# Three column tiles for two products, first keys in two transfers and output weights in ten, in a decoding step with a sliding window

## The chip, the cores and the metric

The kernel runs on one core of a Trainium2 chip. Times are microseconds (us) of the device for one execution. The question is one of some tenths of a microsecond in 191, so a few terms are read from single records of the trace: when an instruction began, when a transfer's packet ran on a DMA engine, when a transfer's completion raised its semaphore. No view of the profile prints these; they were read from the packed traces. Profiled spans are shorter than the timed execution.

## The reference, cut to what matters

```python
def _A_ref(x, k_cache, v_cache, wq, wo):        # x (8, 1, 448), caches (8, 8, 4096, 256)
    W = 1024                                    # window
    q = (x @ wq) ...                            # 16 heads of 256
    k, v = the last W rows of the caches, each of 8 heads used twice
    p = softmax(q k^T / 16);  o = p v
    return o.reshape(8, 1, 4096) @ wo           # wo (4096, 448)
def _B_ref(x, w1, b1, w2, b2):
    return gelu(layernorm(x) @ w1 + b1) @ w2 + b2
g = sigmoid((x * gate_w).sum(-1))
out = g * _A_ref(...) + (1 - g) * _B_ref(...)   # (8, 1, 448), bf16
```

The step reads 77.7 MB and writes 7 KB.

## The kernel before

All large loads go through one ring of nine slots of 2 MB and are issued by SP in one order: query weights, first keys, MLP weights, then keys and values by turns, and the output weights last. The output weights are four quarters, two to a slot. The first three quarters are one transfer each; the last is cut 4+2+2 (of eight row blocks) so that the projection can begin on its first half.

```python
    OT = 4
    DO = D // OT                                              # 112 columns
    WO_PARTS = [[(0, NJ8)]] * (NHQ - 1) + [[(0, 4), (4, 6), (6, 8)]]
    ...
    add_kv("k", A_k_cache, 0)                                 # one transfer of 2 MB
    ...
    for q in range(0, NHQ, 2):
        add(("wo", q), rows_loader(
            [wo_v[:, q + i, j0 * D : j1 * D] for i in range(2) for j0, j1 in WO_PARTS[q + i]]))
    ...
    def tiles(ps):                                            # four column tiles, at partitions 0, 32, 64, 96
        return [(ps[32 * i : 32 * i + NB, :], slice(i * DO, (i + 1) * DO)) for i in range(OT)]
    ...
    def project(q):
        for j in range(NJ8):
            for dst, cols in tiles(A_ps):
                nc.tensor.matmul(dst, lhsT=oP[:, j, q, :], rhs=w[:, o + cols.start : o + cols.stop], ...)
    ...                                                       # spread, values, projection of the quarters
    nc.vector.scalar_tensor_tensor(res[:], in0=A_ps[:], scalar=gg_s[:, 0:1], in1=mixb[:], ...)
    for i, (src, cols) in enumerate(tiles(res)):              # four stores, two by SP and two by ACT
        eng = nc.sync if i % 2 == 0 else nc.scalar
        eng.dma_start(out_f[:, cols], src)
```

Each transfer raises a semaphore when it has landed, and the compiled program hands eight such semaphores to the transfers in turn. And after the last store, the compiled program makes SP wait, one after the other, for all of them, in a fixed order.

Of the kernel before, what the change touches and what calls it, by code (L numbers as in the profile page):

```python
# [11 lines left out]
BF16 = mybir.dt.bfloat16  # L12
# [6 lines left out]
def kernel(  # L19
# [16 lines left out]
    P = nc.NUM_PARTITIONS  # L36

    NB, Sq, D = A_x.shape
# [15 lines left out]
    HH = HD // 2  # L54
    PAIR = 2
    OT = 4
    DO = D // OT
    QN = 512
    QUAD = 4
    RQ = QUAD * rep  # L60
# [7 lines left out]
    HPQ = 4  # L68
    NHQ = Hq // HPQ
    NJ8 = HPQ * NJ  # L70
    WO_PARTS = [[(0, NJ8)]] * (NHQ - 1) + [[(0, 4), (4, 6), (6, 8)]]
    RING = 9
    LAG = 2
    NK = 4
# [10 lines left out]
    consts = ctx.enter_context(tc.tile_pool(name="consts", bufs=1))  # L85
# [23 lines left out]
    def kv_loader(src, u, parts):  # L109
        b, half = divmod(u, Hkv // QUAD)  # L110
        v = src[b, half * QUAD : (half + 1) * QUAD, kv_base:Sk, :].rearrange(
            "a (s c) d -> s a (c d)", c=NCK
        )

        def load(t):
            n = NCK * Dh // parts
            for i in range(parts):
                nc.sync.dma_start(
                    t[:, i * n : (i + 1) * n], v[:, :, i * n : (i + 1) * n]
                )  # L120

        return load

    def rows_loader(pieces):
        def load(t):
            o = 0
            for ap in pieces:
                n = 1
                for s in ap.shape[1:]:
                    n *= s  # L130
                dst = t[:, o : o + n]
                if len(ap.shape) == 3:
                    dst = dst.rearrange("p (a n) -> p a n", a=ap.shape[1])
                nc.sync.dma_start(dst, ap)
                o += n

        return load
# [3 lines left out]
    def add(key, loader):  # L141
        index[key] = len(plan)
        plan.append(loader)

    def add_kv(name, src, u, parts=1):
        add((name, u), kv_loader(src, u, parts))
# [7 lines left out]

    add(("wq", 0), rows_loader([wq_m[:, 0 : 2 * HD]]))
    add(("wq", 1), rows_loader([wq_m[:, 2 * HD : 3 * HD], wq_t]))
    add_kv("k", A_k_cache, 0)
    add(("w1",), rows_loader([w1_m, w1_t]))
    add(("w2",), rows_loader([w2_v]))
    for u in range(1, NQ):  # L160
# [5 lines left out]
    for q in range(0, NHQ, 2):  # L166
# [5 lines left out]
                    for i in range(2)  # L172
                    for j0, j1 in WO_PARTS[q + i]
                ]
# [3 lines left out]
    def slot(*key):  # L178
        return slots[index[key]]

    consts.tile([P, 448], BF16, name="pad")
    x_sb = consts.tile([NB, D], BF16)
    pump()
    nc.scalar.dma_start(x_sb[:], xf)
# [18 lines left out]

    def tiles(ps):
        return [
            (ps[32 * i : 32 * i + NB, :], slice(i * DO, (i + 1) * DO))
            for i in range(OT)
        ]

    xz = consts.tile([NB, 2, P], BF16)  # L210
# [19 lines left out]
    ones_r = consts.tile([1, NB], BF16)  # L230
    mixb = consts.tile([P, DO], F32)
    res = consts.tile([P, DO], BF16)
    nc.vector.memset(spread[:], 0.0)
# [279 lines left out]
    def gather(u):  # L513
        first = soft.pop(u)
        os_ = epool.tile([P, Dh], F32, tag="os", name="os_")
        nc.vector.scalar_tensor_tensor(
            os_[:],
            in0=PO[:, 1, :],
            scalar=own[:, 1:2],
            in1=first[:],  # L520
            op0=ALU.mult,
            op1=ALU.add,
        )
        soft[u] = os_
# [61 lines left out]
    def mlp_out(hs):  # L586
        bb = ps_misc.tile([P, DO], F32, tag="misc", name="bb")
        nc.vector.memset(bb[:], 0.0)
        for c in range(NF):
            w = slot("w2")  # L590
            for dst, cols in tiles(bb):
                nc.tensor.matmul(
                    dst,
                    lhsT=hs[:, c, :],
                    rhs=w[:, c * D + cols.start : c * D + cols.stop],
                    start=(c == 0),
                    stop=False,
                )
        for dst, cols in tiles(bb):
            nc.tensor.matmul(  # L600
                dst, lhsT=ones_r[:], rhs=b2_r[:, cols], start=False, stop=True
            )
        done()
        nc.scalar.activation(mixb[:], bb[:], ACT.Copy, scale=gg_s[:, 1:2])
# [27 lines left out]
    u = NQ - 1  # L632
    A_ps = ps_misc.tile([P, DO], F32, tag="misc", name="A_ps")
    gather(u - 2)
# [32 lines left out]
    def project(q):  # L667
        w = slot("wo", q - q % 2)
        for j in range(NJ8):
            o = ((q % 2) * NJ8 + j) * D  # L670
            for dst, cols in tiles(A_ps):
                nc.tensor.matmul(  # L672
                    dst,
                    lhsT=oP[:, j, q, :],
                    rhs=w[:, o + cols.start : o + cols.stop],
                    start=(q == 0 and j == 0),
                    stop=(q == NHQ - 1 and j == NJ8 - 1),
                )
# [52 lines left out]
```

## Time and profile before

| | before |
|---|---|
| time, median of 3 (later groups: 191.03, 191.20, 191.22, 191.16) | 190.97 us |
| profiled span | 189.4 us |
| DMA queues, mean share of the 16 engines | 97% |
| last piece of output weights lands | 185.18 us |
| result is ready, stores are issued | 186.0 us |

From the page of the kernel before: engines (busy us, share, instructions) and the DMA queues with their packets, MB and share of the 16 engines.

```profile
PE 130.9 (69%) x1022; PEld 66.9 (35%) x1022; DVE 128.0 (68%) x186; ACT 43.2 (23%) x91; POOL 5.0 (3%) x7
...
DMA  6999999999999999999999999999999999999980
...
DMA packets 6590, 77.85 MB, mean 411 GB/s; under 512 B 929, under 2 KB 1330, under 8 KB 1970
...
q1 hardware_dynamic: 6368, 77.67, 96.6%
q8 instruction: 8, 0.13, 0.2%
q10 hardware_dynamic: 210, 0.02, 0.1%
q14 instruction: 4, 0.03, 0.0%
```

The row of digits is the DMA engines' busy share in 40 slices: they are busy throughout, and no other engine is. (PE is TensorE, which does the matmuls, PEld its weight loads, DVE VectorE, ACT ScalarE and POOL GpSimd. SP is SyncE, which in this kernel only issues transfers and waits.) The two "instruction" queues carry the engines' own programs.

From the chain of waits of the kernel before, in order of time (start, duration, what):

```profile
129.78 37.00 DMA slot<-in_A_v_cache_dram
...
166.79 18.39 DMA slot<-in_A_wo_dram
185.18 0.04 issue
185.22 0.39 PE A_ps L672 x6
185.61 0.03 issue
185.63 0.33 DVE res L690
```

The chain stops at 185.96 us, at the last computing instruction. The span ends at 189.4. From the timeline of the kernel before, the stores; and from the list of waits of SP from 185.9 us on (waiter, released by: us in total, times, longest):

```profile
186.00 0.72 SPq L700 DMA_DIRECT2D out_dram<-res  x2
186.00 0.65 ACTq L700 DMA_DIRECT2D out_dram<-res  x2
```

```profile
...
SPq L726 <- DMA out_dram<-res: 1.1, 1, 1.1
SPq L726 <- PEq L726: 0.6, 2, 0.4
```

SP waits once for the stores, for 1.1 us, and twice, for 0.6 us in sum, for the sequencer of PE, the part that issues PE's instructions. From the timeline, PE's last matmuls (in brackets: idle before, and what ended it):

```profile
184.12 0.95 PE L672 MATMUL A_ps<-slot,oP 128*8 128x112 bf16 x24 [0.20 <-DMA slot<-in_A_wo_dram]
185.22 0.36 PE L672 MATMUL A_ps<-slot,oP 128*8 128x112 bf16 x8 [0.16 <-DMA slot<-in_A_wo_dram]
```

PE waits for the weights here, not the other way round.

### The profile page before, as it was taken

Reading aid. Unit: us, or ns where it says so; the run is one execution under the profiler, and the core shown is the slowest. Engines: PE = TensorE matmul, PEld = TensorE weight load, DVE = VectorE, ACT = ScalarE, POOL = GpSimd, SP = SyncE. Lnnn points to the kernel's source line nnn. Section 1 sums busy time; section 2 is a strip of 40 time slices with the busy share of each in tenths; the row PEclk is TensorE's granted clock in tenths of the full one; section 3 lists DMA queues with packets and bytes.
Section 4 is the critical chain, followed back from the end, with each engine's and each line's share of the span. In section 5 each row is a group of like instructions: output and inputs, shape, how many; then the busy total and the mean of one; then the engine's idle time right before and its main releaser. Section 6 shows DMA issues by size and latency. Waiting matters only on the chain.

```text
span 189.4 us, 2510 instructions
## 1 busy us (share of the span) xinstructions
PE 130.9 (69%) x1022; PEld 66.9 (35%) x1022; DVE 128.0 (68%) x186; ACT 43.2 (23%) x91; POOL 5.0 (3%) x7
## 2 busy tenths in 40 slices
PE   0056799795939784899876575859583979399581
PEld 0022754342414241534342323315241524154370
DVE  7841498996949494949593949494958686765310
ACT  2032401214120413040404040404040124004600
POOL 8100000000000000000000000000000000000000
PEclk9999559999996999657999999969998899957955
DMA  6999999999999999999999999999999999999980
GB/s 216 411 443 418 433 431 429 436 419 422 443 433 440 419 419 440 436 436 415 433 436 431 426 422 440 433 436 426 419 440 433 443 422 415 440 433 422 418 338 4
DMA packets 6590, 77.85 MB, mean 411 GB/s; under 512 B 929, under 2 KB 1330, under 8 KB 1970
## 3 DMA queue, kind: packets, MB, share of 16 engines
q1 hardware_dynamic: 6368, 77.67, 96.6%
q8 instruction: 8, 0.13, 0.2%
q10 hardware_dynamic: 210, 0.02, 0.1%
q14 instruction: 4, 0.03, 0.0%
HBM read 77.68 MB, written 0.01 MB: 410 GB/s over the span
## 4 chain that ended last, share of the span: by engine, by line
DMA 70%; DVE 17%; PE 6%; ACT 2%; issue 1%; SPq 0%; ACTq 0%
DMA slot<-in_A_k_cache_dram 41%; DMA slot<-in_A_v_cache_dram 20%; DMA slot<-in_A_wo_dram 10%; DVE kt L357 8%; PE S L429 3%; PE Sq L371 2%; DVE xz L245 1%; ACT qw L412 1%; DVE mx L441 1%; DVE qw L414 1%; ACT qs L381 1%; DVE Sq L198 0%; PE qp L399 0%; PE qt L386 0%; DVE ET L471 0%
## 5 line engine op out<-in xcount | busy, mean ns | idle before, releaser
L357 DVE STREAM_TRANSPOSE kt<-slot 128x2048 int32<-128x2048 int32 x32 | 73.7, 2305 | 33.0 <-DMA slot<-in_A_k_cache_dram 33.0
L429 PE MATMUL S<-kt,qw 128*128 128x512 bf16 x256 | 70.5, 423 | 33.3 <-DVE kt L357 30.7
L429 PEld LDWEIGHTS <-qw 128*128 128x128 bf16 x256 | 26.6, 104 | 73.6 <-issue 52.9
L458 ACT ACTIVATE E<-S,nmx 128x1024 bf16<-128x1024 f32 x16 | 22.2, 1388 | 3.9 <-DVE nmx L455 3.8
L534 ACT CAST oT<-fin 128x16 bf16<-128x16 f32 x16 | 3.6, 227 | 80.5 <-PE fin L531 80.5
L441 DVE TENSOR_REDUCE mx<-S 128x1 f32<-128x1024 f32 x16 | 19.0, 1190 | 0.5 <-PE S L429 0.5
L501 PE MATMUL PO<-slot,ET 128*16 128x512 bf16 x256 | 18.3, 410 | 0.1
L510 ACT ACTIVATE first<-PO,own 128x256 f32<-128x256 f32 x16 | 7.6, 474 | 27.0 <-PE PO L501 26.1
L423 PE MATMUL S<-place,foreign 128*128 128x512 bf16 x32 | 13.0, 407 | 0.1
L471 DVE STREAM_TRANSPOSE ET<-E 128x512 int32<-128x512 int32 x16 | 11.2, 698 | 2.2 <-ACT E L458 2.2
L449 PE MATMUL mz<-m,same 128*128 128x4 f32 x32 | 6.4, 271 | 4.2 <-ACT oT L534 4.1
L482 PEld LDWEIGHTS den<-rowsum,rowden 128*128 128x128 f32 x32 | 6.8, 216 | 3.6 <-issue 1.4
L449 PEld LDWEIGHTS mz<-m,same 128*128 128x128 f32 x32 | 5.2, 203 | 6.1 <-ACT oT L534 5.3
L501 PEld LDWEIGHTS <-ET 128*16 128x16 bf16 x256 | 5.1, 91 | 4.8 <-issue 1.1
L423 PEld LDWEIGHTS <-foreign 128*128 128x128 bf16 x32 | 3.2, 100 | 8.9 <-issue 7.2
L482 PE MATMUL den<-rowsum,rowden 128*128 128x1 f32 x32 | 5.0, 226 | 0.4 <-ACT E L458 0.4
L493 ACT ACTIVATE rsel<-sel,rb 128x8 f32<-128x8 f32 x16 | 4.7, 296 | 1.1 <-DVE rb L492 1.1
L414 DVE CAST qw<-qp 32x512 bf16<-32x512 f32 x4 | 2.7, 687 | 3.1 <-ACT qw L412 3.1
L292 POOL MEMSET qw<- 128x5120 bf16 x1 | 4.4, 4364 | 0.0
L672 PE MATMUL A_ps<-slot,oP 128*8 128x112 bf16 x128 | 3.9, 291 | 0.4 <-DMA slot<-in_A_wo_dram 0.4
L443 DVE TENSOR_SCALAR m<-block,mx 128x4 f32<-128x4 f32 x16 | 3.7, 230 | 0.6
L390 DVE COPY qd<-qt 128x64 bf16<-128x64 bf16 x4 | 0.6, 218 | 4.8 <-PE qt L386 4.8
(135 smaller groups left out, 83.7 us busy)
## 6 DMA issues: line engine op xcount, KB each, us to landing
slot<-in_A_k_cache_dram SPq DMA_DIRECT2D x16, 2048.0 KB, 38.8
slot<-in_A_v_cache_dram SPq DMA_DIRECT2D x16, 2048.0 KB, 36.9
slot<-in_A_wo_dram SPq DMA_DIRECT2D x3, 896.0 KB, 30.7
slot<-in_A_wq_dram SPq DMA_DIRECT2D x1, 2048.0 KB
slot<-in_B_w_dram SPq DMA_DIRECT2D x1, 1568.0 KB
slot<-in_B_w_dram SPq DMA_DIRECT2D x1, 1344.0 KB
slot<-in_A_wq_dram SPq DMA_DIRECT2D x1, 1024.0 KB, 9.5
slot<-in_A_wq_dram SPq DMA_DIRECT2D x1, 512.0 KB, 10.3
```

What stands on the lines that cost most here:

```text
L357: nc.vector.transpose(kt[:].rearrange("p c k x r -> p (c k x r)").bitcast(WORD), kn[:, hf * CH * Dh : (hf + 1) * CH * Dh].bitcast(WORD),)
L414: nc.vector.tensor_copy(dst, src)
L423: nc.tensor.matmul(S[u][:, cols], lhsT=foreign[:], rhs=place[:], start=True, stop=False)
L429: nc.tensor.matmul(S[u][:, cols], lhsT=qw[:, j, u, m * RQ : m * RQ + P], rhs=kt[:, :, k, :, par], start=False, stop=(k == NK - 1 and par = ...
L441: nc.vector.reduce_max(mx[:], S[u][:], axis=AXIS.X)
L449: nc.tensor.matmul(mz[:], lhsT=same[:], rhs=m4[:], start=True, stop=True)
L458: nc.scalar.activation(E[:].rearrange("p c x i -> p c i x"), S.pop(u)[:].rearrange("p (c i x) -> p c i x", i=PAIR, x=BLK), ACT.Exp, bias=n ...
L471: nc.vector.transpose(ET[:].rearrange("p c r i -> p (c r i)").bitcast(WORD), E[:].rearrange("p c x i -> p (c x i)").bitcast(WORD),)
L482: nc.tensor.matmul(den[u][:], lhsT=rowden[:], rhs=rowsum[:], start=True, stop=True)
L493: nc.scalar.activation(rsel[u][:], sel2[:], ACT.Copy, scale=rb[:])
L501: nc.tensor.matmul(PO[32 * t : 32 * t + PAIR * RQ], lhsT=ET[:, c, 0:RQ, :], rhs=vn[:, PAIR * c * Dh : PAIR * (c + 1) * Dh], start=(c < QUA ...
L510: nc.scalar.activation(first[:], PO[:, 0, :], ACT.Copy, scale=own[:, 0:1])
```

## The change

It means to shorten the tail: fewer, wider matmuls, three stores instead of four, and smaller pieces of weights so that PE may begin earlier; and the first keys in halves, so that their first half may be turned (transposed, by DVE) earlier.

```diff
-    DO = D // OT
+    CUTS = (0, 160, 304, D)
+    DO = CUTS[1]
...
-    WO_PARTS = [[(0, NJ8)]] * (NHQ - 1) + [[(0, 4), (4, 6), (6, 8)]]
+    WO_PARTS = [[(0, 4), (4, 8)]] * 2 + [[(0, 4), (4, 6), (6, 8)]] * 2
...
-    add_kv("k", A_k_cache, 0)
+    add_kv("k", A_k_cache, 0, parts=2)
...
-    consts.tile([P, 448], BF16, name="pad")
+    consts.tile([P, 304], BF16, name="pad")
...
-            (ps[32 * i : 32 * i + NB, :], slice(i * DO, (i + 1) * DO))
-            for i in range(OT)
+            (ps[32 * i : 32 * i + NB, 0 : c1 - c0], slice(c0, c1))
+            for i, (c0, c1) in enumerate(zip(CUTS, CUTS[1:]))
```

## The prediction

> **What bounds the kernel.** The transfers do. In the page's slices the 16 DMA engines are 90% busy or more from slice 2 to the last but one, at 415 to 443 GB/s; 77.7 MB come in. The chain of waits is 70% DMA and its end is: last piece of the output weights lands 185.18 us, projection 0.39, result 0.33 (DVE), stores issued at 186.0, span ends at 189.4. PE (69%) and DVE (68%) have slack. So only three places can move the time: bytes per engine, the tail after the last landing, and anything that makes the transfers idle. I see nothing of the third.
>
> **First keys in two.** They land long before they are used: DVE is busy with the query until 24.2 us, when their transposition starts, and it starts without waiting for them. Worth nothing.
>
> **Ten weight pieces instead of six.** The last piece, 224 KB, is the same. The added cuts lie earlier, where PE does not wait for them. They cost packets. Packet durations in the trace: 16384 B 611 ns, 8192 B 309, 7168 B 272, 3584 B 140, 1792 B 74: about 7 ns each beyond the bytes. The Trainium skill (DMA: Bandwidth & Descriptors, "Why small descriptors are slow") names a fixed overhead per packet; the trace agrees. On one engine, packets partly overlap: completions are 2.15 us apart for 8 packets of 7168, and about 1.09 + 0.57 + 0.57 = 2.23 us for a cut 4+2+2. Estimates per engine from these: keys 0.03, quarters cut in two 0.03 each, the third quarter 0.09: about +0.18 us in all, fully on the chain, because all engines share it and the slowest decides. The completion records show that spread: the first of the 16 engines finishes each transfer 1.93 us before the last, and an engine drops 1.42 us back after each 16 KB instruction fetch. The change has 47 fewer matmuls, so the last fetch (184.3 us) may vanish; it was not on the slowest engine, so no gain.
>
> **Three column tiles.** In the tail PE runs at granted clock 0.5 (windows from 180 us). Groups of four 112-column matmuls, which overlap, start 93 ns apart there, 49 ns at full clock: the stream of columns limits, not the instruction count. So three of 160/144/144 should start about 93*160/112 = 133 ns apart (estimate): fewer instructions, but 40 ns more for each of 32 rows of weights, +1.3 us of PE. PE has gaps of 0.2 to 0.5 us before the third quarter and before each piece of the fourth, so most of it hides: my schedule has PE finish the second last piece about 0.1 us before the last lands. On the chain stay the last two groups, 0.36 to 0.40 us. The result is 128x160: from 334 ns (112 columns) and 474 (256) on the same operation, about +0.05. MLP output is off the chain.
>
> **Three stores instead of four.** SP still issues two in a row; ACT's second goes. Perhaps -0.05 to -0.1 in final waits.
>
> **Sum.** +0.18 +0.04 +0.05 -0.07 = +0.2 us: 191.15 us, range 190.8 to 191.6. Faster by over 2%: 0.01; within: 0.98; slower: 0.01.
>
> **What would show it.** Last landing about 185.35 us after; more packets under 2 KB and 8 KB; DMA share unchanged; matmul groups 133 ns apart at clock 0.5 or about 70 at full; no wait of DVE on first keys in either.
>
> **What would make it wrong.** PE falling behind at half clock, so that the last landing no longer releases it (+0.3 to 1 us); a fetch falling on the slowest engine (+1.4 us), or moving off it (-0.2); the shift of constants in memory slowing a PE or DVE operand.

## The result, and the profile after

The changed kernel took 190.53 us in the median of five runs (190.38 to 190.73), beside 191.03 for the kernel before. The ratio is 0.9975 with a 95% interval of 0.9961 to 0.9990: a quarter of a per cent faster. It is the mean time of one kernel's runs over that of the other's of the same rounds, so not quite the ratio of the medians. Two later groups gave 190.54 beside 191.22 (0.9960) and 190.42 beside 191.16 (0.9964). The predicted 191.15 us, with a range of 190.8 to 191.6, lay above it: a small loss was forecast, and a small gain came.

The page of the changed kernel, lines as before:

```profile
PE 134.0 (71%) x975; PEld 69.5 (37%) x975; DVE 128.0 (68%) x186; ACT 43.3 (23%) x91; POOL 5.0 (3%) x7
...
DMA  6999999999999999999999999999999999999990
...
DMA packets 7293, 77.84 MB, mean 412 GB/s; under 512 B 993, under 2 KB 1650, under 8 KB 2546
...
q1 hardware_dynamic: 7088, 77.67, 97.0%
q8 instruction: 7, 0.11, 0.2%
q10 hardware_dynamic: 194, 0.02, 0.1%
q14 instruction: 4, 0.03, 0.0%
```

There are 47 fewer matmuls and yet 3 us more of PE time. The 3 us are not the cost of the wider matmuls alone: b_drain1 below, with the matmuls of the kernel before, shows 133.1 us, 2.2 more than that kernel. There are as many bytes in 703 more packets, and one instruction transfer less. The end of the chain of waits, PE's last matmuls, the stores, and SP's waits from 185.9 us on, of the changed kernel:

```profile
178.83 6.65 DMA slot<-in_A_wo_dram
185.47 0.04 issue
185.52 0.33 PE A_ps L673 x5
185.84 0.03 issue
185.87 0.38 DVE res L691
```

```profile
184.43 0.83 PE L673 MATMUL A_ps<-slot,oP 128*8 128x160 bf16 x18 [0.48 <-DMA slot<-in_A_wo_dram]
185.52 0.30 PE L673 MATMUL A_ps<-slot,oP 128*8 128x160 bf16 x6 [0.26 <-DMA slot<-in_A_wo_dram]
```

```profile
186.28 0.71 SPq L701 DMA_DIRECT2D out_dram<-res  x2
186.29 0.30 ACTq L701 DMA_DIRECT2D out_dram<-res  x1
```

```profile
...
SPq L727 <- DMA out_dram<-res: 0.7, 3, 0.4
SPq L727 <- PEq L727: 0.6, 2, 0.4
```

Up to the stores the changed kernel is *later* by 0.28 us (186.28 against 186.00), about as predicted. That agreement is partly luck: 0.17 us of it is there before the output weights, since the last values ended at 176.32 us in this profile and at 176.15 in the other, and the records below show such a spread in kernels with the same loads. Its span still ends 0.63 us sooner (188.72 against 189.35). The gain lies wholly behind the stores. And SP's waits have changed in kind: one wait of 1.1 us before, three waits of 0.7 us in sum after, each ended by a store.

So I laid out the single records of that stretch. A name such as 104 is a semaphore; "test 104+103" is one of SP's five final waits, with the time at which its record begins. That is when the semaphore named first is raised; where the one named second comes last (a_shift3 and b_tiles3 below), the record lasts until then. The order of the five is the same in every kernel here.

```text
                         before      after       one idle    four loads
                                                 instruction
stores land on           100,102,    106,108,    100,102,    106,105,
                         103,104     110         103,104     110,108
the last lands at        187.791     187.891     187.810     187.711
SP passes test 104+103   187.808     187.041     187.827     186.599
               105+102   188.291     187.110     187.916     187.326
               106+100   188.380     187.512     187.985     187.399
               108+101   188.449     187.709     188.058     187.727
               110+109   188.522     187.908     188.122     187.789
end of the span          189.351     188.721     188.939     188.602
last store to end          1.560       0.830       1.129       0.891
```

(The two right columns are experiments, explained below.) Two things stand out in the column of the kernel before. The last store to land has semaphore 104, which is in the *first* of the five waits; the other four are satisfied by then, but SP must still run through them, at 0.07 to 0.09 us each. And between the first and the second wait SP stands still for 0.48 us (187.808 to 188.291), although both semaphores of the second wait had been raised before. A step from one satisfied wait to the next would have taken 0.09 of these 0.48 us. In the changed kernel the last store has semaphore 110, in the *last* wait, and no such gap lies behind it.

### The profile page after: what moved, and what is told of

The parts are those of the page before. It is cut to its first block, busy times and chain, and to the rows that moved or that the text cites. A ratio compares the mean times of both kernels' runs of the same rounds, so it can differ in the third digit from the quotient of the medians.

```text
span 188.7 us, 2420 instructions
## 1 busy us (share of the span) xinstructions
PE 134.0 (71%) x975; PEld 69.5 (37%) x975; DVE 128.0 (68%) x186; ACT 43.3 (23%) x91; POOL 5.0 (3%) x7
## 4 chain that ended last, share of the span: by engine, by line
DMA 89%; DVE 5%; PE 4%; issue 0%; ACT 0%; SPq 0%
DMA slot<-in_A_k_cache_dram 39%; DMA slot<-in_A_wo_dram 20%; DMA slot<-in_A_v_cache_dram 20%; DMA slot<-in_B_w_dram 6%; DMA slot<-in_A_wq_dram 4%; DVE kt L358 4%; PE S L430 2%; DVE mx L442 1%; PE PO L502 1%; PE fin L532 0%; DVE ET L472 0%; DVE res L691 0%; PE mz L450 0%; DVE os__969 L517 0%; PE A_ps L673 0%
## 5 line engine op out<-in xcount | busy, mean ns | idle before, releaser
L502 PE MATMUL PO<-slot,ET 128*16 128x512 bf16 x256 | 19.8, 437 | 1.4 <-DMA slot<-in_A_v_cache_dram 1.4
L483 PEld LDWEIGHTS den<-rowsum,rowden 128*128 128x128 f32 x32 | 7.3, 232 | 3.7 <-issue 1.4
L673 PE MATMUL A_ps<-slot,oP 128*8 128x144 bf16 (+1 forms) x96 | 4.5, 301 | 0.8 <-DMA slot<-in_A_wo_dram 0.7
```

The lines of the kernel that those rows point to most:

```text
L483: nc.tensor.matmul(den[u][:], lhsT=rowden[:], rhs=rowsum[:], start=True, stop=True)
L502: nc.tensor.matmul(PO[32 * t : 32 * t + PAIR * RQ], lhsT=ET[:, c, 0:RQ, :], rhs=vn[:, PAIR * c * Dh : PAIR * (c + 1) * Dh], start=(c < QUA ...
```

## The experiments

First theory: **the turn of the semaphores**. The change made 49 loads by SP of 44, so the stores' semaphores moved on by five in their turn, and the last store moved from the first wait to the last. Rivals: **fewer stores and wider matmuls**, or **the cuts** of weights or keys, bring the gain by themselves.

Twelve runs were made, in three groups of four, each group on one chip beside the kernel before. The results of all (medians in us; the last column is from the profile):

| run | time | before | ratio, 95% interval | last store to end |
|---|---|---|---|---|
| b_shift4 | 190.44 | 191.20 | 0.9974, 0.9951 to 0.9997 | 0.89 |
| a_shift3 | 190.66 | 191.20 | 0.9973, 0.9962 to 0.9985 | 1.08 |
| b_tiles3 | 190.93 | 191.20 | 0.9991, 0.9979 to 1.0003 | 1.52 |
| b_wo10 | 190.59 | 191.20 | 0.9971, 0.9958 to 0.9984 | 0.84 |
| b_drain1 | 190.73 | 191.22 | 0.9965, 0.9937 to 0.9993 | 1.13 |
| b_drain3 | 190.84 | 191.22 | 0.9969, 0.9943 to 0.9995 | 1.10 |
| b_drain4 | 190.91 | 191.22 | 0.9973, 0.9946 to 0.9999 | 1.10 |
| after_again | 190.54 | 191.22 | 0.9960, 0.9933 to 0.9986 | 0.83 |
| b_k2 | 190.68 | 191.16 | 0.9984, 0.9970 to 0.9998 | 1.04 |
| b_wo16 | 191.07 | 191.16 | 1.0009, 0.9988 to 1.0030 | 0.96 |
| best_t3s5 | 190.22 | 191.16 | 0.9958, 0.9946 to 0.9969 | 0.83 |
| after_third | 190.42 | 191.16 | 0.9964, 0.9953 to 0.9976 | 0.83 |

Single runs 0.7 to 1.7 us above their median occur in three rows (b_shift4, b_k2, b_wo16) and once in the kernel before (192.90, in the group of the idle instructions and after_again); they shift the means, and they widen the intervals. All differences are far below 2%. All outputs were correct.

### b_shift4: the turn of the semaphores alone

The kernel before, with four loads of 32 bytes into unused memory, issued by SP after the last weights:

```diff
+    for i in range(4):
+        nc.sync.dma_start(pad[0:1, 16 * i : 16 * i + 16], B_b2[16 * i : 16 * i + 16].rearrange("(o d) -> o d", o=1))
     HALF = NHQ // 2
```

> The kernel before plus four loads of 32 bytes that nothing reads, issued after the last output weights, so that the four stores use the fifth to eighth of the eight transfer semaphores that are handed out in turn, instead of the first to fourth. Columns, stores, keys and weights are as before. Theory 'turn of the semaphores' (at the end SP waits for the eight in a fixed order; before, the last store to land was in the first wait and four more waits had still to be run through, after the change it was in the last): about 0.6 us faster, 190.3 to 190.6 us; from the last landing of a store to the end of the span 0.77 us instead of 1.50. Rival 'fewer stores or fewer, wider matmuls' and rival 'the cuts of the weights or keys': no change, 190.95 to 191.2 us.

It took 190.44 beside 191.20 us: 0.76 us faster, without any of the four parts of the change. So neither the columns nor the stores nor the cuts are needed for a gain of this size. The end shrank to 0.89 us.

### a_shift3: the changed kernel with the early semaphores

The same loop with three loads in the changed kernel.

> The kernel after plus three such loads of 32 bytes, so that its three stores use the first to third semaphore. Everything else as after. Theory 'turn of the semaphores': it loses the gain, about 191.1 us (190.95 to 191.3), 1.4 to 1.5 us from the last landing of a store to the end of the span. Both rivals: 190.4 to 190.7 us as after.

A miss. It kept its gain: 190.66 us, 0.54 faster than before. The end was 1.08 us, not 1.4 to 1.5: with the stores on early semaphores the four further waits are back (0.25 us), but the standstill of 0.48 us is not (187.596 last landing, first wait's record ends within 0.03 us, then 187.660, 187.733, 187.797, 187.858). The turn of the semaphores explains one part of the end only.

### b_tiles3 and b_wo10: two parts of the change alone

> The kernel before with the three column tiles and three stores alone; the stores use the first to third semaphore. Theory 'turn of the semaphores': no gain, the longer result and matmuls cost 0.05 to 0.15, so 191.0 to 191.25 us. Rival 'fewer stores or matmuls': 190.4 to 190.7 us.

Three tiles and stores alone: 190.93 beside 191.20; ratio 0.9991, an interval that still includes 1. The end is 1.52 us with the standstill in it (first wait's record ends at 187.63, the second begins at 188.072). From the last weights' landing to the last store's landing it took 2.41 us, beside 2.61 before. The stores land 0.18 to 0.21 us one after the other in both, and one store less is worth one such step: from the first issue of a store to the last landing it took 1.60 us beside 1.79. The longer result cost 0.05 us; the last matmuls took 0.06 us less, with PE's clock low at the end of the one profile and full in the other. I had expected no gain. The medians differ by 0.27 us and the means by about 0.17, not clear of the noise; the profiles show the 0.2 us of the store.

> The kernel before with the ten weight pieces alone; four more transfers, so the four stores use the fifth to eighth semaphore. Theory 'turn of the semaphores': -0.6 from the end, +0.15 from the packets, 190.4 to 190.75 us; the weights' last landing 0.1 to 0.2 us later than before. Rival 'cuts bring the gain because PE starts earlier': the same time, but then with the last landing no later and the end of the span as long after the stores as before. Rival 'fewer stores or matmuls': 191.1 to 191.3 us.

Ten pieces alone: 190.59, with an end of 0.84 us and the last landing at 185.446 against 185.184 us. As the theory has it: the gain is in the end, the cuts themselves cost.

### The second theory, and b_drain1, b_drain3, b_drain4

Of the first six profiles, only before and b_tiles3 have the standstill: the two whose SP program has 46 transfers. The others have 50 to 54. On the queue of instructions q14, which brings four pieces of 8192 bytes in every kernel, the last piece follows 0.62 and 0.63 us after the end of the standstill in these two profiles (188.915 and 188.701 us); in the others it has come by 184.3 us. Second theory: **a place in SP's own program**. When SP gets there, it stands still for about half a microsecond, in connection with a fetch of instructions; in the kernel before, that place lies among the final waits, after the last store has landed. Any instruction added to SP ahead of it moves it to where SP waits anyway. The test needs no transfer at all: one idle instruction on SP.

```diff
+    for i in range(1):            # 3, 4
+        nc.sync.drain()           # nothing to wait for on SP
     HALF = NHQ // 2
```

> Revised theory after the first four runs: in the kernel before, SP stands still for 0.48 us at a fixed place of its own program (after its 81st instruction, which is the first of the final waits; a fetch of instructions follows), and there this lies behind the last store. Transfers added earlier on SP push that place back to where SP waits anyway. The semaphore turn is worth only the remaining 0.25 us. This run is the kernel before with one idle instruction on SP ahead of the stores (a drain), no transfer, the same semaphores: the place falls just before the first wait and is hidden. Theory 'place in SP's program': about 0.45 us faster, 190.6 to 190.85 us where before is 191.1 to 191.2; 1.08 us from the last store's landing to the end. Theory 'turn of the semaphores' alone: unchanged, 1.5 to 1.56 us.

It took 190.73 beside 191.22 us: 0.49 us faster for one idle instruction, the same loads, stores, tiles and semaphores. In the table of records above (the column "one idle instruction") the last store lands 0.02 us later than before, the first wait is passed as before, and the second follows after 0.09 instead of 0.48 us. The last piece on q14 now comes at 187.833 us, before the last waits are run through. The end is 1.13 us. The end is thus 0.43 us shorter: the standstill less the ordinary step of 0.09 us, and a few hundredths in the steps behind it. This is the larger part of what the change gained, shown by itself.

> As the run before, with three such idle instructions. Theory 'place in SP's program': the standstill now falls between SP's two stores: the second is issued 0.8 to 0.9 us after the first instead of 0.42, and the time is about that of before, -0.2 to +0.1 us. Theory 'turn of the semaphores': unchanged, 0.42 us between the stores. Rival 'any added instruction helps': as fast as with one.

A miss in its detail: the standstill did not come between the two stores (0.42 us apart, as before), and the time was 190.84, as fast as with one to within the spread. The fetch on q14 lay at 180.42 us, so SP had passed the place well before the stores. The rival, that any added instruction helps, did better here than my count of the instructions.

The count was off by one, and the traces bear the place out. Counting SP's records in them, the standstill of the kernel before lies behind the 79th, the first final wait: 0.455 us from its end to the start of the 80th. In b_tiles3 it is again behind the 79th (0.446 us). In b_wo16, the run with sixteen pieces of weights below, the 79th record is a load in the middle of the stream, and there SP stands still for the same 0.454 us, though the semaphore that the next load waits for had been raised 0.25 us before the end of it. With one idle instruction the 79th record is SP's second store, and SP waits for the landings anyway. With three it is the wait ahead of the first store, where SP waits for the result: hidden, as measured. Two idle instructions would by this count put the standstill between the two stores; that run was not made.

> As the run before, with four idle instructions. Theory 'place in SP's program': the standstill falls before the first store, where SP waits for the result, and is hidden: as with one, about 0.45 us faster than before, and 0.25 us slower than the run with four tiny loads, which has the same length of program but the later semaphores. Theory 'turn of the semaphores': unchanged.

190.91 us and an end of 1.10 us, without a standstill. Against b_shift4, whose SP program has as many instructions but later semaphores, the end is 0.21 us longer (1.10 and 0.89): the part of the semaphores, now by itself. The median is 0.2 us slower than that of b_drain1, with runs from 190.44 to 191.13; the last paragraph of this section says where such a spread comes from.

### b_k2 and b_wo16: keys alone, and the cost of cuts enlarged

> The kernel before with the first keys in two transfers alone. Nothing waits for these keys earlier, their packets cost 0.03 us; but SP has one transfer more (so the standstill is hidden, as with one idle instruction) and the stores use the second to fifth semaphore (the last is in the second final wait, three follow). Expected 0.45 to 0.55 us faster than before, with 1.03 us from the last store's landing to the end of the span. If the keys themselves mattered, the first turn of keys or the first scores would start earlier: they should not (24.2 us). If only fewer stores or weight cuts mattered: no change.

190.68 beside 191.16 us, and an end of 1.04 us, both as expected. The first turn of keys began at 24.42 us (before: 24.21): the half transfers gave it nothing. One transfer on SP was worth half a microsecond, nearly all of it because it is one instruction more: the end is 0.09 us shorter than with the one idle instruction (1.04 and 1.13), as the last store is now in the second wait.

> The kernel before with all four quarters of the output weights in four pieces (16 pieces, packets of 1792 bytes): the suspected cost of the cuts enlarged. From the last value packet to the last weights packet 8.69 us uncut and 8.87 us with ten pieces; with 16 I expect 9.15 to 9.25 us if the cost is per packet. SP is longer by ten transfers (standstill hidden), the stores use the third to sixth semaphore (0.96 us from the last store's landing to the end). Sum: -0.48 -0.13 +0.5, about as before, 191.0 to 191.3 us. Rival 'cuts let PE start earlier and gain': faster than the run with ten pieces.

```diff
-    WO_PARTS = [[(0, NJ8)]] * (NHQ - 1) + [[(0, 4), (4, 6), (6, 8)]]
+    WO_PARTS = [[(0, 2), (2, 4), (4, 6), (6, 8)]] * 4
```

From the end of the last packet of values to the end of the last packet of weights: 8.69 us in the profiles of all eight kernels with six pieces, 8.87 with ten (four profiles), 9.13 with sixteen. So ten pieces cost 0.17 us and sixteen 0.44 (a little less than expected), and the same each time. On each of the 16 DMA engines that is 32 and 80 packets more, 5.4 ns for each in both cases. (In after_again it was 9.159, as a fetch of PE instructions fell on the engine that ended last.) The time was 191.07 us: the cuts had given back what the end had gained.

### best_t3s5 and the changed kernel again

> The changed kernel again, beside the others on one chip. From the terms found so far (weights' packets +0.15, three stores instead of four -0.2, standstill -0.48, semaphores -0.25) it should be 0.6 to 0.8 us faster than before, 190.4 to 190.6 us where before is 191.1 to 191.2; if it is again only 0.5 faster, one of the terms is too large.

> What the terms say is best: three column tiles and stores (-0.2), weights and keys uncut (no packet cost), and five tiny loads that nothing reads, on SP ahead of the stores, so that the standstill is hidden (-0.48) and the stores use the sixth to eighth semaphore (-0.25). Expected 0.85 to 0.95 us faster than before, 190.2 to 190.4 us where before is 191.2, so also faster than after (190.5).

> The changed kernel beside the supposed best on one chip: expected 0.15 to 0.2 us slower than that one (the packets of the cuts), 0.6 to 0.75 us faster than before.

after_again: 0.68 us faster than before; after_third: 0.74. The version put together from the terms (b_tiles3 and five tiny loads on SP) took 190.22 us, 0.94 faster than before and 0.20 faster in the median than the changed kernel beside it. The means of the two (0.9958 and 0.9964) are not apart by their intervals, so that it beats the changed kernel is likely and not shown; the 0.17 us of packets between them is.

What spreads the runs: at the end of the last values, the slowest DMA engine stood anywhere from 175.86 to 176.46 us in the 14 profiles, though the bytes ahead of it are the same. Two causes can be read in the records: the engines take up their first packets at slightly different times in each run (after 7 us they are 0.5 to 0.9 us apart), and an engine that has to bring a 16 KB piece of instructions (q8; by their number PE's) is set back by 1.4 us against the others for the rest of the run. In the kernel before, the gap between the first and the last engine grows from 0.51 us to 1.42, 1.76 and 1.93 us at such fetches. How much each of the two adds to the spread is not shown. A single profile can thus be 0.3 us early or late at the last landing for no reason of the kernel's.

## Why the prediction was wrong, point by point

| term of the prediction | predicted | measured |
|---|---|---|
| first keys in two | +0.03 | nothing starts earlier; packets not separable; one SP instruction more, -0.48 by b_k2 (the standstill, counted in the final waits below) |
| ten weight pieces | +0.15 | +0.17 |
| last matmuls | +0.04 | +0.07 at the low clock, -0.06 at the full one |
| result of 160 columns | +0.05 | +0.05 (0.334 and 0.384 us) |
| three stores | in the term below | -0.2 from one landing less |
| final waits | -0.05 to -0.1, stores included | -0.73 (1.560 to 0.830 us) |
| sum | +0.2 | the rows without the keys: -0.64 to -0.77; timed: -0.5, -0.7, -0.7 in three groups |

- **What bounds the kernel** was right: the transfers, then the tail behind the last landing. (Its figures are read a little off the page: the slices run from 411 GB/s, and the last but one is 80% busy, at 338 GB/s.)
- **The packets** were right in mechanism, and the sum came out in size (+0.15 and +0.17): a packet lasts about 7 ns beyond its bytes, and since packets partly overlap, each one more cost 5.4 ns. The Trainium skill (DMA: Bandwidth & Descriptors, "Why small descriptors are slow (HBM only)") names a fixed overhead per packet; 8.69, 8.87 and 9.13 us for 6, 10 and 16 pieces agree.
- **The matmuls** were right. At the low clock the groups with 160 columns started 133 ns apart where those with 112 had started 93 ns apart. The Trainium skill (TensorE: Matmul & The Clock Gate, "Back-to-back issue gap") gives N/1.2 ns at the cold clock, which is 93 and 133: the trace agrees. PE went on waiting for the weights (0.48 and 0.26 us in the profile after), so of the fewer, wider matmuls only the last groups counted, by the few hundredths in the table, and their sign hung on the clock, which was full there in two profiles of the changed kernel and low in the third.
- **The step that failed** is "SP still issues two in a row; ACT's second goes. Perhaps -0.05 to -0.1 in final waits." I took the 3.4 us behind the result as a fixed cost, less one store, because the chain of waits ends at the last computing instruction. In its place the runs showed three terms. A standstill of SP of 0.48 us lay behind the last landing, and the change moved it away by adding instructions to SP (b_drain1, b_k2); that shortened the end by 0.43 us. The four waits that SP still had to run through, 0.25 to 0.3 us, went because the stores' semaphores moved on in their turn (b_drain4 against b_shift4; a_shift3 against after). And one store less saved a landing of about 0.2 us (b_tiles3). Only the third is what the change was meant to do; the first two come from nothing but the count of its transfers.
- **Listed as what could make it wrong**: PE falling behind, a fetch on the slowest engine, shifted constants. None of the three was it, though the second is real (after_again, where it cost 0.29 us and not the 1.4 that was feared).

What stays open: that the standstill is the fetch of instructions itself is not shown. A piece on q14 follows the 79th record of SP in all fourteen traces, 1.08 to 1.10 us behind it where the loads were over (before, b_tiles3, b_drain1, b_k2) and 1.9 to 4.2 us where they still ran. But the packet itself comes after the standstill has ended (0.62 us in the kernel before), so it is not this packet's end that SP waits for, and why SP stops at this record no run shows. Why the first group gained less than the sum of the terms is open too. The loads that would be needed to place the standstill at will after the last store in the changed kernel were not tried.

## What to carry to other kernels

Read what follows the last computing instruction from the single records, down to the end of the span: which completion the issuing engine tests last, how many satisfied tests it still runs through, and where it stands still with nothing to wait for. When a change adds or removes transfers, it also moves those, by up to 0.7 us here, so before crediting its idea, run a control that adds as many instructions that do nothing. Cuts of a transfer stream that bounds the kernel cost their packets in full, and pay only where something waits for the first piece.

## What the Trainium skill lacked or had wrong

- Runtime: NRT & Kernel Launch, "Instruction fetch mechanics", says of a block boundary that "The cost of crossing a 16 KiB boundary is one DMA tail-bump, mostly hidden." Here one instruction queue moved pieces of 16384 bytes (eight before, seven after 94 PE instructions had gone, so I take them for PE's), the other pieces of 8192, and in the kernel before SP stood still for 0.48 us ahead of such a fetch, wholly exposed at the end; one idle instruction ahead took 0.49 us off the median time. That the fetch is its cause is inferred, as said above.
- The same page does not say what a fetch does to the data: each 16 KB piece set one of the 16 DMA engines back by 1.4 us against the others for the rest of the run, and a load has landed only when its slowest engine is done (spread 0.51 us at the start, 1.93 us at the last values). That a load needs all its engines is as DMA: Bandwidth & Descriptors, "Why a DMA increments its semaphore by 16 and not by 1", has it.
- DMA: Bandwidth & Descriptors, "Specifications", gives 512 bytes as the least transfer for line rate. Packets of 1792 bytes took 74 ns and those of 16384 took 611: 24.2 against 26.8 bytes per ns of an engine, 10% less. In the stream, where packets partly overlap, the loss is smaller: the output weights took 9.13 us all in packets of 1792 bytes and 8.69 us in the six pieces of the kernel before, half of whose packets have 7168, 5% more.
- No page tells of the waits for its transfers with which the compiled program ends, or what one costs: a satisfied wait costs SP 0.06 to 0.09 us, and which of them the last store is in decides how many follow it (end of 1.13, 1.04, 0.96, 0.89 and 0.83 us for the first to the fifth wait, where nothing stands still).
